# Which tiles take two-product values, how output products are shared out, and where a transform's halves stand, in a one-core FNet mixing and ReGLU kernel

## The chip, the cores and the metric

The kernel runs on one core of a Trainium2 chip. The metric is the device time of one execution in microseconds (us). Before the change it is 622.32 us, the median of three runs (622.03 to 622.45).

## What is computed

The input x has 8 batches of 3008 rows with 256 channels. The reference takes a Fourier transform over the rows, a second one over the channels, and keeps the real part. The 24064 rows that result go through a gated network whose hidden width is 1536:

```python
X = np.fft.fft(x, axis=1)
X = np.fft.fft(X, axis=2)
a = X.real.reshape(8 * 3008, 256)
gate = np.maximum(a @ w_gate, 0.0)
val = a @ w_val
out = (gate * val) @ w_out
```

The kernel works in bf16 with fp32 sums.

## The kernel before

**Folding.** The real part of the double transform is a cosine part less a sine part, and two rows that mirror each other differ only in the sign of the sine part. The channel transform is folded into the weights: WA and WB are the gate and value weights (index 0 and 1) seen by the cosine and the sine part, WM is -2 times WB, and WV (written into the unused table kvec) is -0.5 times WM[1]. For each batch GpSimd folds the rows by their symmetries (fold_steps, L224), and 24 matmuls of 376 or 377 columns (dft_steps, L685, and family, L570) give U, the cosine part, and V, the sine part, of half the rows. They fall into four families of six: three matmuls make the odd half, which ScalarE copies (es, L598), three more add the even half to the same bank d, and then ScalarE copies the sum and VectorE makes the difference in two pieces (L601, L603).

**Tiles.** From batch 1 on, the 1505 columns of U and V are cut into three blocks of 512, 512 and 481 columns, and the hidden width into 12 pieces of 128. Each pair of a block and a piece is a tile: 36 in a batch, numbered "at" 0 to 35. A tile makes the gate and the value for its columns (the plus rows) and for their mirrors, and from them two halves of a hidden tile h.

- The gate of an ordinary tile ("n") takes two matmuls: a sine part into bank g (sine_part, L1021), which ScalarE copies (L1024), and a cosine part added to bank p (cosine_part, L1028), into which ScalarE has put channel 128's share (seed, L1016). VectorE makes one gate of the two (both, L1032), GpSimd the other (L1033).
- The gate of a joined tile ("j") has no sine part of its own. ScalarE copies twice the cosine part (copy_cosine, L1039), one slot later the sine part is added to the same bank p (add_sine, L1043), ScalarE copies the sum (L1044), and GpSimd subtracts (L1045).
- The value of an ordinary tile takes three matmuls: two into a bank v (two, L876 and L877), which VectorE multiplies by the relu of the gate (L912), and then the mirror, -2 times the sine part added to the same bank (mirror, L882), after which VectorE multiplies again.
- A short tile has a two-product value: ScalarE seeds bank d (seed_value, L1049), the cosine part is added (value_cosine, L1053), ScalarE copies twice that (L1054), the sine part is added (value_sine, L1058), and the second value is the difference of the copy and the bank. In an "own" short tile VectorE makes the difference in the bank (L1065) and multiplies from there (L912); in the others it makes it in SBUF (L1067) and GpSimd multiplies (L1068), with a relu on ScalarE (L1135).

**Slots.** The order is written out by hand. slot (L1072) issues what is done for one tile: cur, the tile whose value is made; mid, one later; nxt, two later, whose gate is made; after, three later, whose bank is seeded; and pending, one earlier, whose second half is finished. In this order a slot has the sine part of nxt, some output products, the cosine part of nxt, the mirror of pending with its second multiplication, the value of cur with its first multiplication, fold steps on GpSimd, one eviction, and the rest of the output products.

Output products (out_steps, L751; L784) are matmuls of 256 columns that multiply h of the block before by w_out. 24 of them fill a bank o, which ScalarE evicts (L797) and SP stores. Each slot gets per_tile of them, seven or eight, and five eighths stand ahead of the cosine part. A slot's number is corrected: one more if cur is short, one more if pending is, two fewer if mid is, two more if nxt is joined, two fewer if mid is joined.

The lists that hold the rest of the order are DFT_EVEN (L847: how many transform matmuls stand at the end of each slot), the pace of fold steps (L1250), and in the first block of a batch a correction of the products (L1238). Banks: g one, p two, v two, o two, d one, which the transform and the short tiles share.

Of the kernel before, what the change touches and what calls it, by code (L numbers as in the profile page):

```python
# [34 lines left out]
def kernel(  # L35
# [531 lines left out]
    def widen(p, n):  # L567
        nc.tensor.matmul(p[:, n:512], lhsT=WA[0][:, 0:128], rhs=WB[0][:, 0:512 - n], start=False, stop=True, skip_group_check=True)

# [276 lines left out]

    DFT_EVEN = (3, 3, 0) * 4 + (0,) * 24  # L847
    DFT_1 = (3, 0, 3, 0, 0, 0) * 4 + (0, 1, 0, 1, 1) + (0,) * 7
# [10 lines left out]
    def run_one(todo):  # L859
        if todo:  # L860
            todo.pop(0)()
# [135 lines left out]

    def new_tiles():
        for b in range(1, B):
            for blk, block in enumerate(thirds):  # L1000
                for fi in range(NF):
                    st = tile_of(block, fi, uv[b])
                    st["b"] = b
                    mixed = 1 < b < 6 and blk > 0
                    st["kind"] = "o" if (b, blk, fi) == (1, 0, 6) else "j" if mixed and fi in (5, 11) else "n"
                    st["own"] = mixed
                    st["short"] = mixed and fi in (2, 8) or (b, blk) in ((6, 1), (6, 2), (7, 0), (7, 1)) and fi in SHORT or (b, blk) == (7, 2) and fi in (2, 5, 8)
                    st["lead"] = (b, blk, fi) == (1, 0, 0)
                    yield st
# [50 lines left out]
    def value_second(st):  # L1060
        n = st["n"]
        a = st["a"][:, 0:n]
        if st["own"]:
            v = st["v"][:, 0:n]
            nc.vector.tensor_tensor(v, a, v, op=ALU.subtract)  # L1065
            return
        nc.vector.tensor_tensor(a, a, st["v"][:, 0:n], op=ALU.subtract)  # L1067
        nc.gpsimd.tensor_tensor(half_h(st, 1), st["s"][2][:, 0:n], a, op=ALU.mult)  # L1068
        if n == 481:
            keep_rest(st)  # L1070

    def slot(cur, mid, nxt, after, outs, fold_us):  # L1072

        joined, ready = (st is not None and st["kind"] == "j" for st in (nxt, mid))
        outs += 2 * joined - 2 * ready
        outs += cur["short"] + (pending is not None and pending.get("short", False)) - 2 * (mid is not None and mid["short"])
        stop = len(todo_out)

        def out(part):
            run(todo_out, len(todo_out) - stop + outs * part // 8)  # L1080
# [3 lines left out]
        if early:  # L1084
            run_one(turned_out)
            run_one(sums)
            if not todo_dft:
                run_one(sums)
        if old:
# [3 lines left out]
        if new and mid["kind"] != "o":  # L1093
            sine_part(nxt)
        out(4 if lead or nxt is None else 5)
        if new and mid["kind"] == "o":
# [7 lines left out]
        if not lead:  # L1104
            seed(after)
        if pending is not None and pending.get("short"):
            value_second(pending)
        elif pending is not None:
            mirror(pending["v"], pending, 1)
            second(pending)  # L1110
# [8 lines left out]
        else:  # L1119
            relu_mult(cur, 0)  # L1120
        if pending is not None and pending.get("short") and pending["own"]:
            second(pending)
        if lead:
# [15 lines left out]
        if turned_out and not early:  # L1139
            run_one(turned_out)  # L1140
        elif not joined:
            run_one(evict)
# [8 lines left out]
    for b in range(B):  # L1151
# [4 lines left out]
        for blk, block in enumerate(blocks):  # L1156
# [72 lines left out]
            else:  # L1229
                for fi in range(NF):  # L1230
                    at = NF * blk + fi
                    cur = ahead.pop(0)
                    add_h(cur, hs)
                    ahead.append(next(tiles, None))
                    if b < 2:
                        outs = per_tile + ((-2, 0, -2, 2, 2, 0)[fi % 6] if per_tile == 7 else 0)
                    else:
                        outs = per_tile + (0 if blk or b == B - 1 else (-1, -1, 2)[fi % 3])  # L1238
                    if (b, blk) == (B - 1, 2) and fi > 8:
                        outs = (10, 9, 19)[fi - 9]  # L1240
                        if fi == 9:
                            rest = out_steps(b, block, hs)
                            early, rest = rest[:10] + rest[12:16], rest[10:12] + rest[16:]
                            todo_out += early
                    if (b, at) in ((2, 5), (2, 9), (2, 13)):
                        f = slice(128 * (at - 5), 128 * (at - 1))
                        nc.scalar.mul(WV[:, f], WM[1][:, f], -0.5)
                    if (b, at) == (2, 0):
                        nc.sync.dma_start(out=WB[0][0:1, :], in_=WM[0][0:1, :])
                    pending = slot(cur, *ahead, outs, .72 if b < 2 else (.76, .54, .54)[blk])  # L1250
                    for step in more_1.get(at, ()) if b == 1 else ():
                        step()
                    run(todo_dft, DFT_1[at] if b == 1 else DFT_EVEN[at])
            if b or blk > 1:
# [43 lines left out]
```

## Time and profile before

| what | value |
|---|---|
| median of three runs | 622.32 us (622.03 to 622.45) |
| the profiled execution | 621.7 us |
| its span, first to last instruction | 619.6 us |
| TensorE matmul busy, number | 610.7 us, 4032 |
| VectorE busy, number | 549.5 us, 978 |
| ScalarE busy, number | 485.4 us, 911 |
| GpSimd busy, number | 520.5 us, 493 |

The span is that of one execution that was taken by the profiler; 2.1 us of its time lie outside. Rows of a timeline give the start in us, the duration in us, the engine (PE is TensorE's matmul, DVE VectorE, ACT ScalarE, POOL GpSimd), the line of the kernel, the operation, what it writes and reads, the shape, and how many like it follow each other. Rows of groups give, after the bar, the busy time in us, the mean of one in ns, and the idle time ahead of them. A few matmul records are missing from the trace. Matmuls overlap in the records, so that the distance of two starts, not a record's length, is what one takes of the engine.

### The profile page before, as it was taken

To read this page: it belongs to the slowest core of one execution; us is meant where nothing else is said; L and a number is where in the kernel's file an instruction comes from. 1 tells how busy PE (TensorE), PEld (TensorE's weight loads), DVE (VectorE), ACT (ScalarE), POOL (GpSimd) and SP (SyncE) were. 2 spreads that over 40 slices of the span, in tenths; PEclk is the share of its full clock that TensorE was granted. 3 is DMA by queue.
4 is the path that set the end of the run, shared out by engine and by line. 5 is a ranking of instruction groups with operands and counts; after the bars stand their busy time and mean duration, and the time that the engine had idled before them with its cause. 6 is when DMAs were issued, how large, how long until landed. Compare 5 with 4: busy or idle time off the path is not lost.

```text
span 619.6 us, 12415 instructions
## 1 busy us (share of the span) xinstructions
PE 610.7 (99%) x4032; PEld 395.3 (64%) x4076; DVE 549.5 (89%) x978; ACT 485.4 (78%) x911; POOL 520.5 (84%) x493
## 2 busy tenths in 40 slices
PE   8999999999999999999999999999999999999997
PEld 2566666666666666666666666666666666666666
DVE  8886677999899999899999999989999999999991
ACT  7796667776778888778887788777887799999982
POOL 8988992898999989899888988898896588888880
PEclk9999999999999999999999999999999999999999
DMA  9965758735263515524164321621111111211113
GB/s 242 214 199 133 169 175 113 185 75 153 76 152 138 168 52 110 177 76 152 37 159 154 114 94 42 143 70 60 53 44 55 60 44 39 60 52 53 48 47 105
DMA packets 86035, 66.48 MB, mean 107 GB/s; under 512 B 41639, under 2 KB 69063, under 8 KB 85970
## 3 DMA queue, kind: packets, MB, share of 16 engines
q1 hardware_dynamic: 81384, 60.02, 35.5%
q0 software_dynamic: 3984, 4.92, 4.0%
q8 instruction: 32, 0.52, 0.4%
q10 hardware_dynamic: 602, 0.75, 0.3%
q14 instruction: 33, 0.27, 0.2%
HBM read 41.89 MB, written 34.17 MB: 123 GB/s over the span
## 4 chain that ended last, share of the span: by engine, by line
PE 95%; DVE 1%; POOL 1%; issue 1%; DMA 1%; ACT 0%; DVEq 0%; POOLq 0%; ACTq 0%
PE o L784 39%; PE v L877 10%; PE v L882 9%; PE p L1028 8%; PE g L1021 8%; PE v L876 7%; PE d L589 4%; PE p L882 1%; PE d L1058 1%; PE d L1053 1%; PE p L876 1%; PE p L877 1%; DMA XG<-in_x_dram,gidx 1%; PE o L427 1%; PE p L1043 1%
## 5 line engine op out<-in xcount | busy, mean ns | idle before, releaser
L1033 POOL TENSOR_TENSOR r<-r 128x512 f32<-128x512 f32 (+1 forms) x235 | 293.4, 1254 | 75.0 <-DVE r L1032 73.8
L784 PE MATMUL o<-wo,h 128*128 128x256 bf16 x2172 | 328.6, 272 | 0.0
L912 DVE SCALAR_TENSOR_TENSOR h<-r,v 128x512 bf16<-128x512 f32 (+1 forms) x440 | 281.0, 674 | 32.9 <-PE v L882 24.6
L784 PEld LDWEIGHTS <-h 128*128 128x128 bf16 x2220 | 216.7, 98 | 109.8 <-issue 0.9
L1016 ACT ACTIVATE p<-CB,b 128x512 f32<-128x512 bf16 (+1 forms) x251 | 172.4, 687 | 32.1 <-DVE r L1032 28.6
L1024 ACT COPY r<-g 128x512 f32<-128x512 f32 (+1 forms) x235 | 135.9, 578 | 30.8 <-PE g L1021 27.6
L1032 DVE SCALAR_TENSOR_TENSOR r<-r,p 128x512 f32<-128x512 f32 (+1 forms) x235 | 157.4, 670 | 0.8 <-ACT r L1024 0.8
L877 PE MATMUL v<-V,WB 128*128 128x512 bf16 (+3 forms) x265 | 97.0, 366 | 2.2
L1028 PE MATMUL p<-U,WA 128*128 128x512 bf16 (+1 forms) x251 | 94.1, 375 | 0.0
L1021 PE MATMUL g<-V,WM 128*128 128x512 bf16 (+1 forms) x235 | 88.2, 375 | 0.2
L882 PE MATMUL v<-V,WM 128*128 128x512 bf16 (+1 forms) x221 | 82.8, 375 | 0.2 <-DVE h L912 0.2
L876 PE MATMUL v<-U,WA 128*128 128x512 bf16 (+3 forms) x223 | 81.1, 364 | 0.0
L901 DVE TENSOR_TENSOR h<-r,v 128x376 bf16<-128x376 f32 (+2 forms) x90 | 46.1, 546 | 16.4 <-PE v L882 11.3
L797 ACT COPY os<-o 128x512 f32<-128x512 f32 x92 | 52.5, 570 | 2.8 <-PE o L784 2.8
L198 POOL TENSOR_TENSOR XG<-XG,XD 128x510 f32<-128x510 f32 x42 | 52.9, 1271 | 0.9 <-DMA XG<-xr 0.9
L892 ACT ACTIVATE r<-p 128x376 f32<-128x376 f32 (+1 forms) x80 | 38.3, 487 | 18.0 <-PE p L882 8.6
L876 PEld LDWEIGHTS <-WA 128*128 128x128 bf16 x317 | 30.9, 97 | 32.2 <-issue 10.5
L877 PEld LDWEIGHTS <-WB 128*128 128x128 bf16 x317 | 30.9, 97 | 30.1 <-ACT WB L680 0.2
L206 POOL TENSOR_TENSOR AA<-XG 128x510 f32<-128x510 f32 x42 | 45.5, 1094 | 0.0
L912 DVE SCALAR_TENSOR_TENSOR h<-r,d 128x512 bf16<-128x512 f32 (+1 forms) x47 | 31.3, 667 | 0.0
L1028 PEld LDWEIGHTS <-WA 128*128 128x128 bf16 x251 | 24.6, 98 | 3.3 <-issue 0.2
L1021 PEld LDWEIGHTS <-WM 128*128 128x128 bf16 x235 | 23.0, 98 | 5.5 <-issue 0.3
(201 smaller groups left out, 597.3 us busy)
## 6 DMA issues: line engine op xcount, KB each, us to landing
out_dram<-os SPq DMA_DIRECT2D x124, 128.0 KB
xr<-in_x_dram SPq DMA_DIRECT2D x12, 768.0 KB
XG<-xr SPq DMA_DIRECT2D x12, 768.0 KB
XD<-in_x_dram SPq DMA_DIRECT2D x15, 512.0 KB
out_dram<-os SPq DMA_DIRECT2D x35, 112.0 KB
XD<-in_x_dram SPq DMA_DIRECT2D x8, 448.0 KB
CB<-ch SPq DMA_DIRECT2D x7, 376.2 KB
out_dram<-os SPq DMA_DIRECT2D x13, 96.0 KB
```

The source lines that it names most:

```text
L198: e.tensor_tensor(XG[p, r, t, ::-1, 1:D], XG[p, r, t, ::-1, 1:D], XD[p, r, t, :, D - 1:0:-1], op=ALU.add)
L784: nc.tensor.matmul(st["p"][0:m, q, :], lhsT=lhs(f), rhs=wo[:, f, :], start=(f == 0 and not (early and q)), stop=(f == NF - 1), skip_group_ ...
L876: nc.tensor.matmul(bank[:, 0:st["n"]], lhsT=WA[i][:, st["f"]], rhs=st["us"], start=True, stop=False)
L877: nc.tensor.matmul(bank[:, 0:st["n"]], lhsT=WB[i][:, st["f"]], rhs=st["vs"], start=False, stop=True)
L882: nc.tensor.matmul(bank[:, 0:st["n"]], lhsT=W[i][:, st["f"]], rhs=v, start=False, stop=True, skip_group_check=True)
L912: nc.vector.scalar_tensor_tensor(half_h(st, sign), in0=st["s"][1 + sign][:, 0:n], scalar=0.0, in1=st["v"][:, 0:n], op0=ALU.max, op1=ALU.mult)
L1016: nc.scalar.activation(st["p"][:, 0:st["n"]], st["c"], ACTF.Copy, scale=b2[:, st["fi"]:st["fi"] + 1])
L1021: nc.tensor.matmul(st["g"][:, 0:n], lhsT=WM[0][:, st["f"]], rhs=st["vs"], start=True, stop=True)
L1024: nc.scalar.copy(q[:, 0:n], st["g"][:, 0:n])
L1028: nc.tensor.matmul(st["p"][:, 0:n], lhsT=WA[0][:, st["f"]], rhs=st["us"], start=False, stop=True, skip_group_check=True)
L1032: nc.vector.scalar_tensor_tensor(sp[:, 0:n], in0=q[:, 0:n], scalar=-0.5, in1=st["p"][:, 0:n], op0=ALU.mult, op1=ALU.add)
L1033: nc.gpsimd.tensor_tensor(sm[:, 0:n], sp[:, 0:n], q[:, 0:n], op=ALU.add)
```

## The change

Six things change together.

1. The own short tiles of batches 2 to 5 are those with at 9, 13, 17, 21, 25, 29 and 33, seven in a batch; they were pieces 2 and 8 of the second and third block, four in a batch. Batch 6 takes the same seven (not own) for pieces 2, 6 and 10 of its second and third block, six. Batch 7 stays.
2. A tile two behind an own one is joined: seven in each of batches 2 to 5, for four.
3. VectorE's difference of an own tile (own_second) is issued in the tile's own slot, right behind its first multiplication, and the second multiplication comes first on VectorE in the next slot. Both stood in the next slot before, with the first multiplication of that slot's tile between them.
4. The corrections of the output products: one fewer, not two, in the slot ahead of an own tile, and six eighths of them stand ahead of the cosine part there; one more, not two, where nxt is joined. An eviction may now end a slot with a joined nxt.
5. The transform of the next batch takes six matmuls in slots 0, 2, 4 and 6 from batch 2 on, three at the start of the slot and three at its end; it took three at the end of slots 0, 1, 3, 4, 6, 7, 9 and 10. The copy of the odd half follows at once, and both pieces of the difference are issued at the start of the next slot. The products of these slots are corrected by -4 and +3 in turn, and slots 8 to 11 get one more.
6. Smaller ones: WV is made ahead of tiles 1, 3 and 5 of batch 2, the fold steps have another pace by block, and the matmul that fills bank d behind a transform (widen) reads WM[0], not WB[0].

```diff
--- before.py
+++ after.py
@@ -565,7 +565,7 @@
                 todo.pop(0)()
 
     def widen(p, n):
-        nc.tensor.matmul(p[:, n:512], lhsT=WA[0][:, 0:128], rhs=WB[0][:, 0:512 - n], start=False, stop=True, skip_group_check=True)
+        nc.tensor.matmul(p[:, n:512], lhsT=WA[0][:, 0:128], rhs=WM[0][:, 0:512 - n], start=False, stop=True, skip_group_check=True)
 
     def family(b, dst, fam, sine, now=True, pool=None):
 
@@ -844,7 +844,7 @@
 
     DFT_0 = (0, 0, 0, 0, 0, 3, 0, 0, 4, 3, 3, 0), (0, 0, 0, 0, 0) + (1,) * 7, (3, 3, 3, 3, 3, 3, 0, 0, 0, 0, 0, 0)
 
-    DFT_EVEN = (3, 3, 0) * 4 + (0,) * 24
+    DFT_EVEN = (6, 0) * 4 + (0,) * 28
     DFT_1 = (3, 0, 3, 0, 0, 0) * 4 + (0, 1, 0, 1, 1) + (0,) * 7
     todo_out, todo_dft, todo_fold = [], [], []
     credit, paired = 0, False
@@ -996,15 +996,18 @@
     SHORT = (2, 6, 10)
 
     def new_tiles():
+        own = [False] * 2
         for b in range(1, B):
             for blk, block in enumerate(thirds):
                 for fi in range(NF):
                     st = tile_of(block, fi, uv[b])
                     st["b"] = b
-                    mixed = 1 < b < 6 and blk > 0
-                    st["kind"] = "o" if (b, blk, fi) == (1, 0, 6) else "j" if mixed and fi in (5, 11) else "n"
-                    st["own"] = mixed
-                    st["short"] = mixed and fi in (2, 8) or (b, blk) in ((6, 1), (6, 2), (7, 0), (7, 1)) and fi in SHORT or (b, blk) == (7, 2) and fi in (2, 5, 8)
+                    at = NF * blk + fi
+                    two_ = at % 4 == 1 and at > 8
+                    st["kind"] = "o" if (b, blk, fi) == (1, 0, 6) else "j" if own[0] else "n"
+                    st["own"] = two_ and 1 < b < 6
+                    own = own[1:] + [st["own"]]
+                    st["short"] = st["own"] or b == 6 and two_ or (b, blk) in ((7, 0), (7, 1)) and fi in SHORT or (b, blk) == (7, 2) and fi in (2, 5, 8)
                     st["lead"] = (b, blk, fi) == (1, 0, 0)
                     yield st
 
@@ -1060,20 +1063,21 @@
     def value_second(st):
         n = st["n"]
         a = st["a"][:, 0:n]
-        if st["own"]:
-            v = st["v"][:, 0:n]
-            nc.vector.tensor_tensor(v, a, v, op=ALU.subtract)
-            return
         nc.vector.tensor_tensor(a, a, st["v"][:, 0:n], op=ALU.subtract)
         nc.gpsimd.tensor_tensor(half_h(st, 1), st["s"][2][:, 0:n], a, op=ALU.mult)
         if n == 481:
             keep_rest(st)
 
-    def slot(cur, mid, nxt, after, outs, fold_us):
+    def own_second(st):
+        v = st["v"][:, 0:st["n"]]
+        nc.vector.tensor_tensor(v, st["a"][:, 0:st["n"]], v, op=ALU.subtract)
+
+    def slot(cur, mid, nxt, after, outs, fold_us, turned):
 
         joined, ready = (st is not None and st["kind"] == "j" for st in (nxt, mid))
-        outs += 2 * joined - 2 * ready
         outs += cur["short"] + (pending is not None and pending.get("short", False)) - 2 * (mid is not None and mid["short"])
+        soon = mid is not None and mid["own"]
+        outs += joined - 2 * ready + soon
         stop = len(todo_out)
 
         def out(part):
@@ -1084,15 +1088,16 @@
         if early:
             run_one(turned_out)
             run_one(sums)
-            if not todo_dft:
-                run_one(sums)
+            run_one(sums)
+            run(todo_dft, turned // 2)
+            run_one(turned_out)
         if old:
             gate(nxt)
         lead = cur["lead"]
         out(4 if lead else 0)
         if new and mid["kind"] != "o":
             sine_part(nxt)
-        out(4 if lead or nxt is None else 5)
+        out(4 if lead or nxt is None else 5 + soon)
         if new and mid["kind"] == "o":
             sine_part(nxt)
         if ready:
@@ -1103,7 +1108,9 @@
             copy_cosine(nxt)
         if not lead:
             seed(after)
-        if pending is not None and pending.get("short"):
+        if pending is not None and pending.get("own"):
+            second(pending)
+        elif pending is not None and pending.get("short"):
             value_second(pending)
         elif pending is not None:
             mirror(pending["v"], pending, 1)
@@ -1118,8 +1125,8 @@
             mult(cur, 0, cur["first"])
         else:
             relu_mult(cur, 0)
-        if pending is not None and pending.get("short") and pending["own"]:
-            second(pending)
+        if cur["own"]:
+            own_second(cur)
         if lead:
             out(5)
             cosine_part(nxt)
@@ -1138,7 +1145,7 @@
         run_fold(fold_us)
         if turned_out and not early:
             run_one(turned_out)
-        elif not joined:
+        else:
             run_one(evict)
         if not early:
             run_one(sums)
@@ -1235,22 +1242,22 @@
                     if b < 2:
                         outs = per_tile + ((-2, 0, -2, 2, 2, 0)[fi % 6] if per_tile == 7 else 0)
                     else:
-                        outs = per_tile + (0 if blk or b == B - 1 else (-1, -1, 2)[fi % 3])
+                        outs = per_tile + (0 if blk or b == B - 1 else (-4, 3, -4, 3, -4, 3, -4, 3, 1, 1, 1, 1)[fi])
                     if (b, blk) == (B - 1, 2) and fi > 8:
                         outs = (10, 9, 19)[fi - 9]
                         if fi == 9:
                             rest = out_steps(b, block, hs)
                             early, rest = rest[:10] + rest[12:16], rest[10:12] + rest[16:]
                             todo_out += early
-                    if (b, at) in ((2, 5), (2, 9), (2, 13)):
-                        f = slice(128 * (at - 5), 128 * (at - 1))
+                    if (b, at) in ((2, 1), (2, 3), (2, 5)):
+                        f = slice(256 * (at - 1), 256 * (at + 1))
                         nc.scalar.mul(WV[:, f], WM[1][:, f], -0.5)
                     if (b, at) == (2, 0):
                         nc.sync.dma_start(out=WB[0][0:1, :], in_=WM[0][0:1, :])
-                    pending = slot(cur, *ahead, outs, .72 if b < 2 else (.76, .54, .54)[blk])
+                    pending = slot(cur, *ahead, outs, .72 if b < 2 else (.78, .52, .5)[blk], DFT_EVEN[at])
                     for step in more_1.get(at, ()) if b == 1 else ():
                         step()
-                    run(todo_dft, DFT_1[at] if b == 1 else DFT_EVEN[at])
+                    run(todo_dft, DFT_1[at] if b == 1 else DFT_EVEN[at] // 2)
             if b or blk > 1:
                 run(todo_out, len(todo_out))
             if blk == len(blocks) - 1 or (b, blk) == (0, 1):
```

## The prediction

> **What bounds the kernel now.** I read the page first, then the timeline of TensorE (PE) in the middle of batch 5, then VectorE's (DVE) beside it, and last the groups by line that carry the terms of the sum.
>
> ```profile
> span 619.6 us, 12415 instructions
> ...
> PE 610.7 (99%) x4032; PEld 395.3 (64%) x4076; DVE 549.5 (89%) x978; ACT 485.4 (78%) x911; POOL 520.5 (84%) x493
> ...
> PEclk9999999999999999999999999999999999999999
> ...
> PE 95%; DVE 1%; POOL 1%; issue 1%; DMA 1%; ACT 0%; DVEq 0%; POOLq 0%; ACTq 0%
> ```
>
> TensorE is the bound: it holds 95% of the chain that ended last, and its granted clock is full (9 or more tenths) in every slice. Its busy share says less, since the ends of matmuls are modelled. What counts is the distance from one start to the next. Here is one slot (the work that is issued for one tile) and the start of the next:
>
> ```profile
> 421.42 0.38 PE L1028 MATMUL p<-U,WA 128*128 128x512 bf16 x1
> 421.63 0.38 PE L882 MATMUL v<-V,WM 128*128 128x512 bf16 x1
> 422.06 0.38 PE L877 MATMUL v<-V,WB 128*128 128x512 bf16 x1
> 422.28 0.49 PE L784 MATMUL o<-wo,h 128*128 128x256 bf16 x3
> 422.61 0.38 PE L1021 MATMUL g<-V,WM 128*128 128x512 bf16 x1
> 422.82 0.49 PE L784 MATMUL o<-wo,h 128*128 128x256 bf16 x3
> 423.15 0.38 PE L1028 MATMUL p<-U,WA 128*128 128x512 bf16 x1
> 423.46 0.38 PE L882 MATMUL v<-V,WM 128*128 128x512 bf16 x1
> 423.67 0.38 PE L876 MATMUL v<-U,WA 128*128 128x512 bf16 x1
> 423.89 0.38 PE L877 MATMUL v<-V,WB 128*128 128x512 bf16 x1
> 424.10 0.38 PE L1053 MATMUL d<-U,WA 128*128 128x512 bf16 x1
> ```
>
> From 423.46 to 424.10 three 512-wide matmuls start 0.64 us apart in all, 0.215 us each, though a record lasts 0.38. Three output products (L784) take 0.33 us, 0.11 each. (At 421.63 the record of L876 is missing; the distance to L877 is that of two.) So the engine is packed, with one exception: the mirror (L882) follows the cosine (L1028) after 0.21 us at 421.42, but after 0.31 us at 423.15. That is a stall of 0.09 us. VectorE explains it:
>
> ```profile
> 422.12 1.28 DVE L912 SCALAR_TENSOR_TENSOR h<-r,v 128x512 bf16<-128x512 f32 x2
> 423.32 0.68 DVE L1032 SCALAR_TENSOR_TENSOR r<-r,p 128x512 f32<-128x512 f32 x1
> 423.94 1.28 DVE L912 SCALAR_TENSOR_TENSOR h<-r,v 128x512 bf16<-128x512 f32 x2
> ```
>
> The mirror adds to the bank that the second of two L912 has just read. That pair begins 0.48 us after a mirror's start (423.46, then 423.94) and takes 1.28; it ends at 423.40, and the mirror starts 0.06 later. So two mirrors cannot start closer than 0.48 + 1.28 + 0.06 = 1.82 us. Between the two mirrors shown TensorE has five 512s and six output products, 5 x 0.215 + 6 x 0.11 = 1.73: 0.09 short, as seen. Only six products stand there because the slot before a two-product tile gives up two of its eight. The same stall stands at all 16 two-product tiles of batches 2 to 5; the first and the last:
>
> ```profile
> 205.40 0.38 PE L1028 MATMUL p<-U,WA 128*128 128x512 bf16 x1
> 205.71 0.38 PE L882 MATMUL v<-V,WM 128*128 128x512 bf16 x1
> ...
> 457.47 0.37 PE L1028 MATMUL p<-U,WA 128*128 128x481 bf16 x1
> 457.75 0.36 PE L882 MATMUL v<-V,WM 128*128 128x481 bf16 x1
> 457.95 0.36 PE L876 MATMUL v<-U,WA 128*128 128x481 bf16 x1
> ```
>
> They are 0.31 and 0.28 us where 0.215 and 0.20 (457.75 to 457.95, 481 wide) would do: 0.09 and 0.08 lost.
>
> **Part 1: more two-product tiles.**
>
> ```profile
> L1058 PE MATMUL d<-V,kvec 128*128 128x512 bf16 (+1 forms) x31 | 11.6, 374 | 0.0
> ```
>
> ```profile
> L1065 DVE TENSOR_TENSOR d<-r,d 128x512 f32<-128x512 f32 (+1 forms) x16 | 10.8, 672 | 0.0
> ```
>
> There are 31 such tiles now, 16 of them "own" ones, whose second half is made on VectorE. By the new rule there are 28 own ones (seven in each of batches 2 to 5), seven in batch 6 for six, and nine in batch 7 as before: 44, so 13 matmuls go. Nine are 512 wide (two in each of four batches and one in batch 6), four are 481 wide: 9 x 0.215 + 4 x 0.20 = 2.74 us. All of it is on the path, because TensorE is.
>
> The Trainium skill (TensorE: Matmul & The Clock Gate, Back-to-back issue gap) states a sustained spacing of about 131 ns for 512 columns in a stream of weight loads and matmuls. By that the 13 would be worth only 1.7 us, and the time a microsecond longer than my sum. The rows above, which are such a stream, show 215, and the measurement decides.
>
> Every own tile also brings a joined gate two tiles on, 12 more of each. VectorE gains one L1065 and loses one L1032 for each pair (0.67 and 0.68 us): nothing. GpSimd has a subtraction in place of an addition: nothing. ScalarE gains three instructions, a seed, a doubled copy and a second gate copy, some 0.6 us each: 12 x 3 x 0.6 = 22 us on 485.4. That is 82% of the span, hidden as long as no single copy comes late (below).
>
> **Part 2: the shares of output products.** The slot before an own tile (T-1) now gives up one product, not two, and puts six eighths of its seven ahead of the cosine. Between its mirror and the one before stand three left over, five in front, and five 512s: 1.075 + 8 x 0.11 = 1.95 us, over 1.82. The stall goes: 16 x 0.09 = 1.44 us. The same sum for the own tile's slot T is 1.95 again: two products left over and six in front, and five 512s (the mirror, two values, the own tile's cosine value, the gate's cosine; the joined gate has no sine there). For ordinary slots it is 1.95 too. The own tile has no mirror. Batch 6 keeps its stalls, since only own tiles get the correction.
>
> What is late next? There are two candidates, both behind an own tile.
>
> (a) *VectorE.* From T's mirror to the next one (two slots on) VectorE has five in a row: second(T-1), first(T), the difference, second(T), first(T+1). With 0.60 from start to start (1.28 - 0.68) that is 0.48 + 4 x 0.60 + 0.68 + 0.06 = 3.62 us; TensorE has, in order, the mirror, T's sine value, four products, a sine, four products, the joined sine, a cosine, two values, three products, a sine, five products and a cosine: 9 x 0.215 + 16 x 0.11 = 3.70. So 0.08 us of room. But second(T) now stands right behind the difference that it reads. What a dependent neighbour costs:
>
> ```profile
> 5.88 0.29 DVE L385 TENSOR_SCALAR qd<-dvec,ums 128x129 f32<-128x129 f32 x1
> 6.21 0.23 DVE L386 TENSOR_SCALAR qd<-qd 128x129 f32<-128x129 f32 x1
> ```
>
> The second starts 0.04 us after the first has ended, where independent ones overlap by 0.08: 0.12 us more. The stall is then 0.12 - 0.08 = 0.04 in each of 28 slots, 1.1 us; with no such cost it is nothing. The Trainium skill (VectorE: DVE Perf Modes, The DRAIN you can't avoid) says that a semaphore between two VectorE instructions costs nothing extra, as the next waits for the pipe anyway. By that, (a) would be nothing; the rows show overlap without a wait and none with one.
>
> (b) *ScalarE.* The bank of the joined gate is free for a new seed only after its second copy:
>
> ```profile
> 428.88 0.38 PE L1043 MATMUL p<-V,WB 128*128 128x512 bf16 x1
> ```
>
> ```profile
> 429.30 0.59 ACT L1044 COPY r<-p 128x512 f32<-128x512 f32 x1
> 429.92 0.69 ACT L1016 ACTIVATE p<-CB,b 128x512 f32<-128x512 bf16 x1
> ```
>
> From the joined sine to the end of that seed are 429.92 + 0.69 - 428.88 = 1.73 us. The next cosine comes after five 512s and eight products, 1.95 us (one mirror less than now): 0.2 us of room. It is gone when an eviction stands ahead of the copies:
>
> ```profile
> L797 ACT COPY os<-o 128x512 f32<-128x512 f32 x92 | 52.5, 570 | 2.8 <-PE o L784 2.8
> ```
>
> One comes for each 24 products, so in every third slot: nine of 28 own tiles. It pushes the copies back by the part of its 0.57 us that still runs when the sine is there, by my estimate about half, 0.3, which is 0.1 over the room: 0.9 us. Bounds for (a) and (b) together are 0 and 2.0 us. I take 0.8, nearer to the low end, because a stall of one kind uses up the room of the other, and because an eviction often falls into an idle stretch.
>
> **Part 3: the transform.** It has 24 matmuls a batch before and after; only their places change: a family in one slot of two, three at each end, instead of three in two slots of three.
>
> ```profile
> 468.09 0.64 PE L589 MATMUL d<-tabS,G 128*128 128x376 bf16 x3
> 468.57 0.38 PE L1021 MATMUL g<-V,WM 128*128 128x512 bf16 x1
> ```
>
> ```profile
> L603 DVE SCALAR_TENSOR_TENSOR V<-es,d 128x188 bf16<-128x188 f32 x24 | 8.2, 342 | 0.0
> ```
>
> Three take 0.48 us. A slot with six and three products is 1.075 + 0.96 + 0.33 = 2.37 us, the next with ten products 2.18: 4.55 together. VectorE has six of 0.60 and both sums, 2 x 0.34, which is 4.28. Between the halves a copy must run:
>
> ```profile
> L598 ACT COPY es<-d 128x377 f32<-128x377 f32 (+1 forms) x30 | 14.2, 474 | 5.1 <-PE d L589 4.0 <-PE d L586 0.9
> ```
>
> The five 512s and three products of the slot, 1.4 us, cover its 0.47; uncovered, 20 families (four in each of batches 2 to 6) would cost 9 us. So nothing is gained or lost. Two row loads on SP's queue ride on the transform's 22nd step and come four slots earlier; the sums that they wait for end a slot before them in both orders. The three scalings of value weights (L1247) stand earlier in batch 2, the same three; no transfer is added. The folds on GpSimd are paced a little differently, with the same steps. The 135-column matmul that fills up a bank (widen, L568) reads another tensor of the same size: nothing.
>
> **Sum.** -2.74 - 1.44 + 0.8 = -3.4 us. The profiled execution took 621.7 us, 2.1 of it outside its span of 619.6; it would take 618.3. Its median over three runs is 622.32, 0.6 above; I predict 618.9 on that scale. With the unknown at its ends: 618.1 and 620.1.
>
> **Rivals.**
> - *The stalls move, and only the products are gained.* (a) and (b) at their upper ends and some of the old stalls left: -2.74 + 0 to 1.2, so 619.6 to 620.8. For it speaks the small room of 0.08 and 0.2 us; against it, that these are the only two places under 0.3.
> - *ScalarE becomes the bound behind each joined gate (slower).* If an eviction or other copy stood ahead of the two copies at every own tile with its full 0.57 us, it would exceed the room by 0.37 at 28 places: 10.4 us, 622.32 - 4.2 + 10.4 = 628.5. It turns the sign from 4.2 / 0.37, 12 places, on. Against it: evictions come in one slot of three, and ScalarE is at 78%.
> - *The change does not do what it says*: the products go, but TensorE then waits elsewhere for the same time, VectorE being packed in stretches. Then nothing that can be told from no change: 622.32 within 1.24, 621.1 to 623.6. Against it: VectorE has 3 x 0.60 = 1.8 us in every slot, TensorE 1.74 in one slot of four and 1.84 to 2.06 in the others.
>
> **How the numbers follow.** The forecast has 0.70, the first rival 0.15, the third 0.08, the slower one 0.07. A difference of 0.2% (1.24 us) is about what a measurement of this kernel can tell from no change. Faster gathers the first two and a little of the third, 0.86; same 0.07; slower 0.07. The range 617.8 to 620.9 holds the forecast with its bounds (a few tenths of measurement beneath) and the first rival, 0.85 in all.
>
> **What would show it.** The number of sine values (L1058 in this page) goes to 44 and that of differences to 28. In the slot before an own tile the mirror starts 0.21 us after the cosine. Two slots after an own tile's mirror the next may be late by up to 0.06, and a cosine by 0.1 after an eviction. It is wrong if a cosine waits for a seed at most own tiles, if the transform's second half waits for the copy, or if mirrors stall in the slots with ten products.

## The result and the profile after

The changed kernel takes 620.75 us (median of 12 runs, 620.43 to 621.2) against 622.16 us (12 runs, 621.8 to 622.52) on the same chip: a ratio of 0.9977, 95% interval 0.9969 to 0.9984. That is 1.4 us faster. I had forecast 3.4 us. The time lies in the range that I gave, but under half of the gain came.

The page after, as far as it answers to the lines shown of before:

```profile
span 619.1 us, 12491 instructions
...
PE 612.8 (99%) x4063; PEld 394.4 (64%) x4063; DVE 552.8 (89%) x978; ACT 507.5 (82%) x950; POOL 522.1 (84%) x494
...
PE 93%; DMA 2%; POOL 2%; DVE 1%; issue 1%; ACT 0%; POOLq 0%; DVEq 0%; ACTq 0%
```

TensorE still bounds the kernel; ScalarE has the 22 us more that 12 pairs of an own and a joined tile, and one tile of batch 6, bring (485.4 to 507.5). The page counts more matmuls than before (4063 for 4032) only because records are missing from the trace of before; the weight loads (PEld), of which this page has one for each matmul, fell from 4076 to 4063, by 13. The groups show the tiles that were meant:

```profile
L1073 DVE TENSOR_TENSOR d<-r,d 128x512 f32<-128x512 f32 (+1 forms) x28 | 18.9, 676 | 0.0
...
L1061 PE MATMUL d<-V,kvec 128*128 128x512 bf16 (+1 forms) x44 | 16.5, 374 | 0.0
```

There are 28 own tiles and 44 two-product tiles, for 16 and 31, so 13 matmuls are gone. Where the rest of the gain went stands in TensorE's timeline of the changed kernel. Line 1031 is now the cosine and 1024 the sine; the first rows are two slots behind own tile 13 of batch 5, the last two are the slot ahead of own tile 17:

```profile
426.36 0.71 PE L784 MATMUL o<-wo,h 128*128 128x256 bf16 x5
426.90 0.38 PE L1031 MATMUL p<-U,WA 128*128 128x512 bf16 x1
427.25 0.38 PE L882 MATMUL v<-V,WM 128*128 128x512 bf16 x1
427.47 0.38 PE L876 MATMUL v<-U,WA 128*128 128x512 bf16 x1
...
428.99 0.38 PE L1031 MATMUL p<-U,WA 128*128 128x512 bf16 x1
429.20 0.38 PE L882 MATMUL v<-V,WM 128*128 128x512 bf16 x1
```

The stall ahead of an own tile is gone, as forecast: cosine to mirror is 0.21 us at 428.99. But two slots behind an own tile the distance is 0.35 us, at 426.90, a stall of 0.13. VectorE in the same stretch:

```profile
423.92 0.69 DVE L912 SCALAR_TENSOR_TENSOR h<-r,v 128x512 bf16<-128x512 f32 x1
424.52 0.68 DVE L912 SCALAR_TENSOR_TENSOR h<-r,d 128x512 bf16<-128x512 f32 x1
425.12 0.69 DVE L1073 TENSOR_TENSOR d<-r,d 128x512 f32<-128x512 f32 x1
425.91 0.69 DVE L912 SCALAR_TENSOR_TENSOR h<-r,d 128x512 bf16<-128x512 f32 x1
426.52 0.68 DVE L912 SCALAR_TENSOR_TENSOR h<-r,v 128x512 bf16<-128x512 f32 x1
```

These are the five in a row of my sum. The starts are 0.60 us apart, except behind the difference (L1073): 0.79 us. The second multiplication reads what the difference has just written, and starts 0.10 us after its end, where instructions that do not wait overlap by 0.09. The same 0.10 stands at all 28 own tiles. The last of the five ends at 427.20, and the mirror starts at 427.25.

The other new stall is behind tiles 21 and 33 of each of these batches, four times each. ScalarE, then TensorE, behind tile 21 of batch 5:

```profile
440.16 0.59 ACT L797 COPY os<-o 128x512 f32<-128x512 f32 x1
440.63 0.57 ACT L1027 COPY r<-g 128x481 f32<-128x481 f32 x1
441.08 0.61 ACT L1047 COPY r<-p 128x512 f32<-128x512 f32 x1
441.73 0.67 ACT L1019 ACTIVATE p<-CB,b 128x481 f32<-128x481 bf16 x1
```

```profile
441.77 0.71 PE L784 MATMUL o<-wo,h 128*128 128x256 bf16 x5
442.44 0.36 PE L1031 MATMUL p<-U,WA 128*128 128x481 bf16 x1
```

The eviction (L797) stands ahead of the two copies (L1027 and L1047), the seed (L1019) ends at 442.40, and the cosine starts at 442.44 in place of 442.31 (441.77 and five products of 0.11): 0.13 us late. Behind tile 33 it is 0.18.

The table sums TensorE's stalls by place in batches 2 to 5: the distance from one matmul's start to the next, less what its width takes (0.2155, 0.203 and 0.109 us for 512, 481 and 256 columns). It has rows for the experiments too.

| kernel | mirror ahead of an own tile | mirror two slots behind one | cosine behind 21 and 33 | other | sum, us |
|---|---|---|---|---|---|
| before | 1.49 | 0 | 0 | 0.16 | 1.65 |
| after | 0 | 2.12 | 1.25 | 0.02 | 3.39 |
| e6_old_shares | 2.02 | 0.45 | 0.34 | 0.01 | 2.82 |
| e4_no_evict | 0 | 2.74 | 0 | 0.02 | 2.75 |
| e11_no_dep_psum | 0 | 0 | 1.20 | 0.26 | 1.46 |
| e12_sine_first | 0 | 0 | 1.22 | 0.01 | 1.23 |
| e13_sine_first_no_evict | 0 | 0 | 0 | 0 | 0 |

After the change the second column has 22 places: ten of 0.13 us, eight of 0.075 (481 columns) and four of 0.05 behind tile 21, where the late cosine covers the rest. Behind tile 33 it covers the whole, and behind tile 9 the mirror is late in two batches of four.

So the books of the change: 13 matmuls, -2.75 us; stalls in batches 2 to 5, +1.74; the other batches nearly nothing. That makes -1.0. In the traces the time from the first seed of batch 1 to the end of the span went from 521.3 to 520.2 us, and the medians say -1.4 (interval -1.0 to -1.9). The 0.4 between the books and the medians stays open; the smaller edits of point 6 were not run alone.

### The profile page after: what moved, and what is told of

It is laid out like the page before. It is cut to its first block, busy times and chain, and to the rows that moved or that the text cites. A ratio compares the mean times of both kernels' runs of the same rounds, so it can differ in the third digit from the quotient of the medians.

```text
span 619.1 us, 12491 instructions
## 1 busy us (share of the span) xinstructions
PE 612.8 (99%) x4063; PEld 394.4 (64%) x4063; DVE 552.8 (89%) x978; ACT 507.5 (82%) x950; POOL 522.1 (84%) x494
## 4 chain that ended last, share of the span: by engine, by line
PE 93%; DMA 2%; POOL 2%; DVE 1%; issue 1%; ACT 0%; POOLq 0%; DVEq 0%; ACTq 0%
PE o L784 39%; PE v L882 9%; PE p L1031 9%; PE v L877 8%; PE v L876 8%; PE g L1024 8%; PE d L589 4%; DMA wo<-in_moe_w_out_dram 2%; PE d L1056 1%; PE d L1061 1%; PE p L882 1%; PE p L1046 1%; PE p L876 1%; PE p L877 1%; POOL h L342 1%; POOL XG L120 1%
## 5 line engine op out<-in xcount | busy, mean ns | idle before, releaser
L1036 POOL TENSOR_TENSOR r<-r 128x512 f32<-128x512 f32 (+1 forms) x223 | 278.8, 1255 | 70.9 <-DVE r L1035 69.9
L912 DVE SCALAR_TENSOR_TENSOR h<-r,v 128x512 bf16<-128x512 f32 (+1 forms) x414 | 265.9, 675 | 25.2 <-PE v L882 17.0
L1019 ACT ACTIVATE p<-CB,b 128x512 f32<-128x512 bf16 (+1 forms) x251 | 172.7, 688 | 29.4 <-DVE r L1035 25.4
L1035 DVE SCALAR_TENSOR_TENSOR r<-r,p 128x512 f32<-128x512 f32 (+1 forms) x223 | 149.7, 671 | 0.8 <-ACT r L1027 0.8
L1027 ACT COPY r<-g 128x512 f32<-128x512 f32 (+1 forms) x223 | 129.1, 579 | 10.6 <-PE g L1024 7.7
L877 PE MATMUL v<-V,WB 128*128 128x512 bf16 (+3 forms) x252 | 92.1, 366 | 0.0
L876 PE MATMUL v<-U,WA 128*128 128x512 bf16 (+3 forms) x252 | 92.1, 365 | 0.0
L882 PE MATMUL v<-V,WM 128*128 128x512 bf16 (+1 forms) x208 | 77.9, 374 | 0.2 <-DVE h L912 0.2
L797 ACT COPY os<-o 128x512 f32<-128x512 f32 x92 | 53.0, 576 | 2.8 <-PE o L784 2.8
L912 DVE SCALAR_TENSOR_TENSOR h<-r,d 128x512 bf16<-128x512 f32 (+1 forms) x72 | 48.4, 672 | 2.9
L876 PEld LDWEIGHTS <-WA 128*128 128x128 bf16 x304 | 29.6, 97 | 32.8 <-issue 11.3
L1048 POOL TENSOR_TENSOR r<-r 128x512 f32<-128x512 f32 (+1 forms) x28 | 35.1, 1252 | 2.2 <-ACT r L1047 1.6
L598 ACT COPY es<-d 128x377 f32<-128x377 f32 (+1 forms) x30 | 14.2, 475 | 19.5 <-PE d L589 18.6
```

The costliest lines, as they stand in the source:

```text
L797: nc.scalar.copy(os_[0:m, 0:len(some)], st["p"][0:m, 0:len(some)])
L876: nc.tensor.matmul(bank[:, 0:st["n"]], lhsT=WA[i][:, st["f"]], rhs=st["us"], start=True, stop=False)
L877: nc.tensor.matmul(bank[:, 0:st["n"]], lhsT=WB[i][:, st["f"]], rhs=st["vs"], start=False, stop=True)
L882: nc.tensor.matmul(bank[:, 0:st["n"]], lhsT=W[i][:, st["f"]], rhs=v, start=False, stop=True, skip_group_check=True)
L912: nc.vector.scalar_tensor_tensor(half_h(st, sign), in0=st["s"][1 + sign][:, 0:n], scalar=0.0, in1=st["v"][:, 0:n], op0=ALU.max, op1=ALU.mult)
L1019: nc.scalar.activation(st["p"][:, 0:st["n"]], st["c"], ACTF.Copy, scale=b2[:, st["fi"]:st["fi"] + 1])
```

## The experiments

Each run's ratio is to runs of the kernel before on the same chip (622.1 to 622.2 us). The changed kernel is at 620.75, with a ratio of 0.9969 to 0.9984; where a run's interval overlaps with this one, what tells the two apart is the sums of stalls in the traces, of one execution each.

**e1_second_later.** The first theory to test: the mirrors behind own tiles are late because of the wait for the difference.

```diff
-        if pending is not None and pending.get("own"):
-            second(pending)
...
             relu_mult(cur, 0)
+        if pending is not None and pending.get("own"):
+            second(pending)
```

> The changed kernel, with the second multiplication of an own tile issued one place later on VectorE: behind the first multiplication of the next tile, not ahead of it. My theory: the mirrors two slots behind an own tile (0.13 us late at 512 columns, 0.07 at 481, 2.1 us in all) are late because the second multiplication waits for the difference just ahead of it and pushes the next tile's first multiplication back. Then these stalls go: 620.75 - 2.1 = 618.6 us. Rival (the mirror waits for something else, such as its bank or ScalarE): stalls and time stay, 620.7.

Measured: 620.61 us (ratio 0.9976, 0.9966 to 0.9986). The time stayed, yet not for the rival's reason. The late mirrors did go; others came. VectorE behind tile 17 of batch 3, then TensorE in the slot ahead of that tile:

```profile
288.08 0.69 DVE L1073 TENSOR_TENSOR d<-r,d 128x512 f32<-128x512 f32 x1
289.05 0.69 DVE L912 SCALAR_TENSOR_TENSOR h<-r,v 128x512 bf16<-128x512 f32 x1 [0.28 <-PE v L877]
```

```profile
284.15 0.38 PE L1031 MATMUL p<-U,WA 128*128 128x512 bf16 x1
284.44 0.38 PE L882 MATMUL v<-V,WM 128*128 128x512 bf16 x1
```

What stands behind the difference now waits 0.28 us for a value that TensorE has not made yet, so VectorE loses more than the 0.19 of before. Mirrors ahead of own tiles are late by 0.07 to 0.12 again, sine values by 0.08, and the seeds behind tiles 21 and 33 by 0.18 and 0.24: 3.35 us of stalls in batches 2 to 5 for 3.39. My expectation missed that the multiplication put in front has a wait of its own.

**e2_no_read.** This takes the wait away without moving anything.

```diff
     def second(st):
+        if st.get("own"):
+            st["v"] = st["a"]
         (relu_mult if "s" in st else mult)(st, 1)
```

> The changed kernel, with the second multiplication of an own tile reading ScalarE's doubled copy in place of the difference (so 28 tiles' second halves are computed from another tensor); every instruction stays where it was. My theory (the wait of an instruction for its neighbour's result): it starts 0.60 us after the difference, not 0.79, and the mirrors are not late, 618.6 us. Rival (five VectorE instructions in a row are simply too many for the 3.7 us): the stalls stay at about 0.13, 620.7.

Measured: 626.13 us (ratio 1.0067, 1.0051 to 1.0082), far slower than either theory. VectorE, then GpSimd behind tile 25 of batch 3:

```profile
305.29 0.66 DVE L1075 TENSOR_TENSOR d<-r,d 128x481 f32<-128x481 f32 x1
305.85 1.68 DVE L912 SCALAR_TENSOR_TENSOR h<-r 128x481 bf16<-128x481 f32 x1
307.45 0.65 DVE L912 SCALAR_TENSOR_TENSOR h<-r,v 128x481 bf16<-128x481 f32 x1
```

```profile
305.33 1.68 POOL L213 TENSOR_TENSOR F<-AA 128x768 bf16<-128x768 f32 x1
306.96 1.62 POOL L1050 TENSOR_TENSOR r<-r 128x481 f32<-128x481 f32 x1
```

The multiplication follows the difference after 0.56 us, without the wait, but takes 1.68 us where the same work with one operand in PSUM takes 0.65. Its operands now both lie in SBUF, and GpSimd runs beside it, itself 1.62 us on what takes 1.21. Over all 28 it is 0.68 to 1.77 us. In each of the 28 places a GpSimd instruction was running when the multiplication began, and the multiplication ended 0.52 to 0.60 us after that instruction's end, whether 0.08 or 1.25 us of it were left (here L213 ends at 307.01 and the multiplication at 307.53). So it waits for that instruction. The time says nothing on the rivals, since the run brought a larger cost of its own. The Trainium skill (SBUF — State Buffer, Who interferes with whom) states that a VectorE instruction with two SBUF inputs contends with a GpSimd instruction that reads SBUF; this trace agrees, on both engines.

**e3_diff_sbuf.** Whether the wait is longer because the result lies in PSUM. Its expectation was written before e2 was measured, and it has the same flaw.

```diff
-        nc.vector.tensor_tensor(v, st["a"][:, 0:st["n"]], v, op=ALU.subtract)
+        a = st["a"][:, 0:st["n"]]
+        nc.vector.tensor_tensor(a, a, v, op=ALU.subtract)
+        st["v"] = st["a"]
```

> The changed kernel, with the difference of an own tile written to SBUF, over ScalarE's doubled copy, and the second multiplication reading it there. If the wait is longer because the result goes through PSUM (0.10 us after the end, where SBUF's neighbours at the start of the kernel showed 0.04), the stalls fall by 0.06 in 24 to 28 places, 1.5 us: 619.2. If a wait for a neighbour costs the same in both memories, nothing moves: 620.7.

Measured: 631.08 us (ratio 1.0146, 1.013 to 1.0161). The multiplication has two operands in SBUF again, and takes 1.07 us in the mean. The question can still be read from the rows of VectorE:

```profile
283.28 0.68 DVE L1074 TENSOR_TENSOR r<-r,d 128x512 f32<-128x512 f32 x1
284.07 1.63 DVE L912 SCALAR_TENSOR_TENSOR h<-r 128x512 bf16<-128x512 f32 x1
```

From the difference in SBUF to its reader are 0.79 us, 0.11 after its end by these rounded rows: the wait is the same in both memories. What the kernel's start had shown, 0.04, holds for its short instructions of 129 columns and not here.

**e11_no_dep_psum.** The mended form of e2: the multiplication reads the bank itself, and nothing reads the difference.

```diff
-        nc.vector.tensor_tensor(v, st["a"][:, 0:st["n"]], v, op=ALU.subtract)
+        a = st["a"][:, 0:st["n"]]
+        nc.vector.tensor_tensor(a, a, v, op=ALU.subtract)
```

> The changed kernel, with the difference of an own tile written to SBUF where nothing reads it, and the second multiplication reading the bank itself (so 28 tiles' second halves are computed from the first value). Order and operands' memories stay; only the wait for the neighbour's result is gone, and unlike in the run that read the doubled copy the second multiplication has one operand in PSUM. The wait theory: the multiplication starts 0.60 us behind the difference, not 0.79, the late mirrors two slots behind an own tile (0.13 and 0.07 us) go, and the time falls by 2.1 us to 618.6. Rival (five VectorE instructions are too many in any case): the stalls stay, 620.7.

Measured: 618.92 us (ratio 0.9949, 0.9934 to 0.9964), 1.8 less than the changed kernel. VectorE:

```profile
423.22 0.68 DVE L1074 TENSOR_TENSOR r<-r,d 128x512 f32<-128x512 f32 x1
423.81 0.68 DVE L912 SCALAR_TENSOR_TENSOR h<-r,d 128x512 bf16<-128x512 f32 x1
424.41 0.68 DVE L912 SCALAR_TENSOR_TENSOR h<-r,v 128x512 bf16<-128x512 f32 x1
```

0.59 us in place of 0.79, with the same instructions in the same order. None of the mirrors two slots behind an own tile is late. The rival, that five instructions are too many, falls.

**e12_sine_first.** An order with no neighbour to wait for: in an own tile's slot the sine value stands ahead of the mirror of the tile before, and that tile's second multiplication comes between the difference and its reader.

```diff
+        if cur["own"]:
+            value_sine(cur)
+            relu_mult(cur, 0)
+            own_second(cur)
         if pending is not None and pending.get("own"):
             second(pending)
```

(The three calls at their old place are left out for an own tile.)

> The changed kernel with another order in an own tile's slot: TensorE's sine value ahead of the mirror of the tile before, and on VectorE first multiplication, difference, the other tile's second multiplication, so that one instruction stands between the difference and the multiplication that reads it, and none waits for a value that is not there. The wait theory: the late mirrors go, 618.6 us. Rival (VectorE has no slack around an own tile, and what is won comes back at the next mirror, as when the second multiplication was put later): 620.7.

Measured: 618.68 us (ratio 0.9944, 0.993 to 0.9957). VectorE in the stretch that was shown of the changed kernel:

```profile
422.15 0.69 DVE L912 SCALAR_TENSOR_TENSOR h<-r,d 128x512 bf16<-128x512 f32 x1
422.76 0.69 DVE L1073 TENSOR_TENSOR d<-r,d 128x512 f32<-128x512 f32 x1
423.35 0.68 DVE L912 SCALAR_TENSOR_TENSOR h<-r,v 128x512 bf16<-128x512 f32 x1
423.95 0.68 DVE L912 SCALAR_TENSOR_TENSOR h<-r,d 128x512 bf16<-128x512 f32 x1
424.55 0.68 DVE L912 SCALAR_TENSOR_TENSOR h<-r,v 128x512 bf16<-128x512 f32 x1
```

Five in a row again, 0.60 apart all of them.

**e4_no_evict.** The other new stall.

```diff
             run_one(turned_out)
-        else:
+        elif not joined:
             run_one(evict)
```

> The changed kernel, with no eviction in the slot of an own tile, as before the change; it goes to the next slot. My theory: the eight cosines that start late by 0.13 (behind tile 21) and 0.18 us (behind tile 33) wait for a seed that an eviction pushed back; 1.25 us of stall go, but the late mirrors right behind them, which they had covered in part, come out: some 0.6 us back. 620.1 us. Rival (the seed is late by the two copies alone): the cosines stay late, 620.7.

Measured: 619.98 us (ratio 0.9965, 0.9951 to 0.9979), as expected, though the interval overlaps with that of the changed kernel. No cosine waits for a seed any more; the mirrors that these stalls had covered come out, 2.74 us for 2.12. Behind tile 21 nothing is won: the mirror is now 0.18 us late, which is what the cosine (0.13) and the mirror (0.05) lost before. The gain comes from tile 33, where 0.18 becomes 0.025.

**e13_sine_first_no_evict.** Both edits.

> The run before (sine value first) and no eviction in an own tile's slot. By the wait theory and the one on evictions both kinds of stall go, 2.1 and 1.25 us: 617.4. If VectorE has no slack: 620.0, as with the eviction moved alone.

Measured: 617.3 us (ratio 0.9921, 0.9907 to 0.9935). ScalarE and TensorE behind tile 21 of batch 5:

```profile
437.77 0.58 ACT L1047 COPY r<-p 128x512 f32<-128x512 f32 x1
438.39 0.67 ACT L1019 ACTIVATE p<-CB,b 128x481 f32<-128x481 bf16 x1
439.00 0.58 ACT L797 COPY os<-o 128x512 f32<-128x512 f32 x1
```

```profile
438.74 0.71 PE L784 MATMUL o<-wo,h 128*128 128x256 bf16 x5
439.29 0.37 PE L1031 MATMUL p<-U,WA 128*128 128x481 bf16 x1
```

The eviction comes behind the seed, which ends at 439.06, and the cosine starts at once after its five products. No stall over 0.012 us is left in batches 2 to 5.

**e6_old_shares.** What the even shares of output products are worth by themselves.

```diff
-        outs += joined - 2 * ready + soon
+        outs += 2 * joined - 2 * ready
...
-        out(4 if lead or nxt is None else 5 + soon)
+        out(4 if lead or nxt is None else 5)
```

> The changed kernel with the old shares of output products: two fewer in the slot ahead of an own tile, five eighths ahead of the cosine, two more where nxt is joined. By my sum the mirrors ahead of own tiles are 0.09 us late again, 28 times, 2.5 us, but the stalls two slots behind own tiles shrink by the one product that moves behind the own tile's mirror (0.11 us each, 1.9 us in all): 621.3. Rival (the shares do no more than move one product, and no stall hangs on them): 620.7.

Measured: 620.14 us (ratio 0.9969, 0.9957 to 0.9981): some 0.6 faster than the changed kernel, with intervals that overlap, where I had expected 0.6 slower and the rival no difference. TensorE, two slots behind an own tile and then ahead of the next:

```profile
426.12 0.38 PE L1031 MATMUL p<-U,WA 128*128 128x512 bf16 x1
426.36 0.38 PE L882 MATMUL v<-V,WM 128*128 128x512 bf16 x1
...
427.87 0.38 PE L1031 MATMUL p<-U,WA 128*128 128x512 bf16 x1
428.18 0.38 PE L882 MATMUL v<-V,WM 128*128 128x512 bf16 x1
```

The stalls are where I put them: some 0.08 to 0.12 ahead (22 places, not 28: none ahead of tile 9, and ahead of tile 13 in two batches of four), 0.02 to 0.06 behind. What I left out is the third place: the product that moves behind the own tile also gives the seeds time, and those stalls fall from 1.25 to 0.34 us. Together 2.82 for 3.39, 0.57 less, which fits the difference of the medians.

**e15_fewer_tiles.** What one matmul is worth, in a kernel without stalls.

```diff
-                    two_ = at % 4 == 1 and at > 8
+                    two_ = at % 6 == 1 and at > 8
```

> The run with the sine value first and the eviction moved, where TensorE has no stall in batches 2 to 5, with four two-product tiles in each of batches 2 to 6 (13, 19, 25 and 31) in place of seven. It measures what a matmul taken away is worth: 15 come back, ten of 512 columns and five of 481. At the distance of two starts in the trace (0.215 and 0.20 us) that is 3.15 us, less three stalls of 0.09 in batch 6: 617.3 + 2.9 = 620.2. At 0.131 us each: 617.3 + 2.0 - 0.3 = 619.0.

Measured: 620.92 us (11 runs, ratio 0.9981, 0.9972 to 0.999), 3.6 more than the 617.3 of e13. The stalls did not fall by the 0.3 us that I expected: batch 6 has four where e13 has six, which is 0.17 less, but in one slot of batch 7 VectorE begins some 0.35 late in this trace, which does not show why, and all stalls of batches 2 to 7 together rise by 0.2. So the 15 matmuls are worth 3.4 us, or 3.8 if that one late slot is no part of the other executions: 0.23 to 0.25 each, give or take 0.07 by the two intervals. The 0.21 that their widths make in the mean is inside, 0.131 is not.

**e9_no_tile9** and **e10_no_tile9_old_dft.** Whether the transform's new places matter. A seed of tile 9 uses the bank that the old places hold until slot 11, so both do without that tile (`at > 12`); e10 has the old places besides, with the old order of their copies and the old correction of the products.

> The changed kernel without a two-product tile in the first block (no tile 9 in batches 2 to 6): five matmuls come back, 1.08 us, and two late mirrors of 0.13 go: 620.75 + 0.8 = 621.55. It is the partner of the next run, in which the transform could not stand beside a seed of tile 9.

> The run without tile 9, with the old places of the transform (three matmuls at the end of slots 0, 1, 3, 4, 6, 7, 9 and 10) and the old correction of the products. My sum has the new places at nothing: the same time as the run without tile 9, 621.5, or 0.1 to 0.2 more for the late mirrors at the start of batches 2, 4 and 6. Rival (the new places bring or cost something that the others hid): over 0.5 us apart.

Measured: 622.15 and 622.27 us, with intervals of the ratio of 0.9991 to 1.0009 and 0.9992 to 1.001. They are 0.12 apart, as expected; the intervals would hide a difference of up to some 0.6. Both are some 0.6 above the 621.5 that I had set. Half of that stands in the trace of e9: the two late mirrors behind tile 9 go (0.27 us), but in one slot of batch 2 and one of batch 5 VectorE begins late, for a reason that the trace does not show, and costs 0.24 and 0.11, so that the stalls of batches 2 to 5 are 3.45 for 3.39. For the rest, some 0.3, I have no cause to show; it is less than the interval.

**e14_and_shares_all.** The best kernel so far with the even shares around the tiles of batches 6 and 7 too.

```diff
-        soon = mid is not None and mid["own"]
-        outs += joined - 2 * ready + soon
+        soon = mid is not None and mid["short"]
+        outs += joined - 2 * ready + soon - (cur["short"] and not cur["own"])
```

> The run with the sine value first and the eviction moved, and the shares of output products evened out around the 16 other two-product tiles too (batches 6 and 7: one fewer, not two, in the slot ahead, six eighths of them ahead of the cosine, and one fewer in the tile's own slot). Theory (a mirror is late where less than 1.82 us of TensorE's work lies between it and the one before): some 15 stalls of 0.09 us in batches 6 and 7 go, 1.3 us: 616.0. Rival (these tiles' difference, which VectorE makes for GpSimd, and the relu on ScalarE leave no slack): 617.3.

Measured: 616.96 us (ratio 0.9918, 0.9905 to 0.9932), 0.3 less than e13, with intervals that overlap. The stalls of batches 6 and 7 fall from 1.53 to 0.84 us, not to nothing: most are 0.034 where they were 0.09, and near the end two sines and one mirror are late by 0.06 and 0.11 more.

## What the prediction had right, and the step that failed

- *The products: right.* 13 matmuls went, nine and four by width as counted, at 0.215 and 0.20 us. Batches 2 to 5 balance with this price, and e15 excludes 0.131.
- *The stalls ahead of own tiles: right in itself, wrong as a gain.* All of them went. But by the stalls of e6 the even shares, taken alone, cost 0.6 us in this kernel, since the product that they move is missing behind the own tile, where two other waits are short of time. I took the removed stall as a term of its own and did not carry the moved product into the room of (a) and (b).
- *(a), the second multiplication behind its difference: the right place and mechanism, the wrong size.* This is the step that failed, and most of what the allowance of 0.8 missed. I priced the wait for a neighbour at 0.12 us, from two instructions of 129 columns at the start; at 512 columns it is 0.19 (0.79 less 0.60), in all 28 places. The room was 0.06, not 0.08, since a product takes 0.109 us and not the 0.11 of my sum. That makes a stall of 0.13 and not 0.04, or 2.12 us in 22 places for the 1.1 at my upper end. Small errors in the price and the room make three times the stall, because the room takes the first part off. e11 and e12 take the wait away, and the stalls with it.
- *(b), the eviction ahead of the seed: right in place and number, too small.* Eight places where I had nine, 0.13 and 0.18 us where I had 0.1, 1.25 in all for 0.9. e4 takes them away, and half comes back as late mirrors.
- *The allowance of 0.8 us between bounds of 0 and 2.0.* The two together are 3.37. I argued for the low end because stalls would share their room; e4 shows that they do (0.6 comes back), but not nearly enough. The bound of 2.0 was no bound, since it took my estimates of both prices for ends.
- *The transform: right*, nothing, as far as e9 and e10 can tell without tile 9.
- *The rival that fits best* is the first: the stalls move. It was priced with 0 to 1.2 us of new stalls beyond the old; 1.74 is what came in batches 2 to 5.
- *That the time lies in the range is in part luck.* The kernel before came out at 622.16 us here, not the 622.32 that I started from. As a gain, 1.41 us stands at the small end of the range (622.32 - 620.9 = 1.42), and 0.4 of it is not in the books.

## What to carry to other kernels

Where one engine is packed and another feeds it with less than a tenth of a microsecond to spare, a change is judged by the room at each wait after the change, not by the stall that it removes: work that fills one hole leaves another. Put an independent instruction between one that writes and one that reads its result on VectorE, and see that the one put there has no wait of its own: e1 and e12 each put one there, and lie 1.9 us apart. An experiment that changes an operand's memory changes more than the wait.

## What the hardware showed

- Of two VectorE instructions of 512 fp32 columns, the second starts 0.09 us before the end of the first when it does not read the result and 0.10 after it when it does: 0.19 us a pair, the same in all 28 pairs, for a result in PSUM and in SBUF (e3) alike. The prediction set a rule of the Trainium skill (VectorE: DVE Perf Modes, The DRAIN you can't avoid), by which the wait is free, against a row that showed 0.12; these runs show 0.19.
- A VectorE multiplication of two fp32 operands in SBUF took 0.68 to 1.77 us (e2) at the same place where one with an operand in PSUM takes 0.68; it ended 0.52 to 0.60 after the GpSimd instruction that was running when it began. GpSimd's subtractions there rose in the mean:

```profile
L1048 POOL TENSOR_TENSOR r<-r 128x512 f32<-128x512 f32 (+1 forms) x28 | 35.1, 1252 | 2.2 <-ACT r L1047 1.6
```

That is the changed kernel; with the difference in SBUF (e3) it is

```profile
L1048 POOL TENSOR_TENSOR r<-r 128x512 f32<-128x512 f32 (+1 forms) x28 | 40.8, 1456 | 1.6 <-ACT r L1047 1.5
```

1.46 us where it was 1.25.
